# The second layer's activation as two ScalarE passes and one VectorE pass, without a maximum

## The chip, the cores and the metric

The kernel runs on one core of one Trainium2 chip. The metric is the device time of one execution in microseconds (us). Each time is that of a whole execution; the profiled execution also has a span, from its first to its last instruction.

## The reference

Three layers follow each other: an attention with pooled keys and values, and two layers that each multiply, apply an activation and multiply again. The change touches the activation of the last one:

```python
def _moe2_ref(x, w_in, w_out):          # x: 4608 x 512
    h = x @ w_in                        # w_in: 512 x 2048
    beta = 1.0
    neg = h <= -beta
    pos = h >= beta
    g = np.where(pos, h, np.where(neg, 0.0, (h + beta) ** 2 / (4.0 * beta)))
    return (g @ w_out).astype(np.float32)   # w_out: 2048 x 512
```

So g is h above 1, zero below -1 and ((h + 1) / 2) squared between. Inputs and output are fp32; the weights of both layers come as 64-bit numbers and are turned into fp32 in the kernel.

## The kernel before

Every operand of a matmul is split into a high part, a copy rounded to the matmul's format (ScalarE), and a low part, source minus high part (VectorE); a product is then three matmuls: high by high, high by low, low by high. Attention and the first layer take the first 960 us or so, and the second layer's second product (w_out, L1080) the last 380. The change lies in the stage between them, `first_phase` of the class `Second`, which forms h = x @ w_in and g.

That stage splits the matrices into 2 x 2 blocks and forms the four blocks of h from seven products instead of eight. It runs over 6 panels p of 768 tokens and, in each, over 8 steps j of 128 columns from each half of w_in: 48 steps s, one per **cycle**. A cycle has seven **slots**, each with one product of six 128x384 matmuls (line 838), in the order 6, 1, 7, 5, 2, 4, 3. Products 6, 5 and 3 belong to step c, the other four to step c + 1.

Three PSUM banks collect them. **X** takes products 1 and 2 and is one block of h. **V** takes product 7, which is copied out as p7 (`p<-V`), and then product 4. **Y** starts as a copy of X after product 1; product 6 is added and the sum copied out as `q`; product 5 is added, and then VectorE forms the block **W** = Y + p7 in p7's tile (`p<-Y,p`, line 857); product 3 is added and Y is a block of h. VectorE forms the block V = V + q in q's tile (`q<-V,q`, line 857). So product 3 has to wait until W has been formed, with products 2 and 4 (two slots) between, and product 5 until q has been copied.

The activation of one 128x384 block runs in up to four steps, in one tile t: `act1` (ScalarE, line 871) forms max(h/2 + 1/2, 0), with the constant tile `half` as bias. For X and Y, `act2` forms min(t, 1) times t on VectorE (line 877). For V and W, `act2` takes the minimum on GpSimd (line 879) and `act3` the square on ScalarE (line 884). `act4` (VectorE, line 890) takes the maximum of h and t, and the tile is stored to DRAM as g.

The order is written out by hand: after each slot's product, `after(c, slot)` issues its copies, adds and activation steps, and then a plan by cycle and slot issues the other work of that slot. That work is: the splits of the next panel's operands (`parts`, high part line 698, low part line 699) and the sums and differences of them (line 756), in the last three cycles of each panel and the first of the next (5 to 8, 13 to 16 and so on); and the splits of w_out's blocks (`w2o`), seven at a time over cycles 1 and 2, 3 and 4, 9 and 10, and so on up to 27 and 28. Every engine runs its instructions in this order, so one that waits holds all that are behind it. All transfers go through SyncE's queue, in the same order.

Of the kernel before, what the change touches and what calls it, by code (L numbers as in the profile page):

```python
# [8 lines left out]
F32 = mybir.dt.float32  # L9
F32R = mybir.dt.float32r  # L10
U32 = mybir.dt.uint32
AF = mybir.ActivationFunctionType
ALU = mybir.AluOpType
# [4 lines left out]
P = 128  # L18
# [17 lines left out]
def attention_moe_moe2(ctx: ExitStack, tc: tile.TileContext, qT, kT, v, k01, v01, w_in1, w_out1, w_in2, w_out2, out):  # L36
# [5 lines left out]
    nc = tc.nc  # L42
# [12 lines left out]
    const = ctx.enter_context(tc.tile_pool(name="const", bufs=1))  # L55
# [8 lines left out]
    ps_a = ctx.enter_context(tc.tile_pool(name="ps_a", bufs=2, space=PSUM))  # L64

    ident = const.tile([P, P], F32, name="ident")
    half = const.tile([P, 1], F32, name="half")
    mask = const.tile([96, 4], F32, name="mask")


# [128 lines left out]
    class Attention:  # L199
# [176 lines left out]
        def scores_early(self, blk, hf, ti, tag):  # L376
# [31 lines left out]
            for _ in range(4):  # L408
                next(parts)
# [257 lines left out]
    class Second:  # L667
# [26 lines left out]
            self.plan.setdefault((cycle, slot), []).append((f, args))  # L694


        def parts(self, hi, lo, src, engine=nc.vector):
            nc.scalar.activation(out=hi, in_=src, func=AF.Copy)
            engine.tensor_tensor(out=lo, in0=src, in1=hi, op=ALU.subtract)  # L699

        def w1_load(self, j):
            x, y = (raw_tile([P, DM], F32, f"w1{n}{j}") for n in "xy")
# [165 lines left out]
        def act1(self, what, s):  # L868
            if 0 <= s < self.STEPS:
                t = self.kept["t", what, s] = self.t_tile(f"t{what}{s}")  # L870
                nc.scalar.activation(out=t, in_=self.h_of(what, s), func=AF.Relu, scale=0.5, bias=half)  # L871

        def act2(self, what, s):
            if 0 <= s < self.STEPS:
                t = self.kept["t", what, s]
                if what in "XY":
                    nc.vector.scalar_tensor_tensor(out=t, in0=t, scalar=1.0, in1=t, op0=ALU.min, op1=ALU.mult)
                else:
                    nc.gpsimd.tensor_scalar(out=t, in0=t, scalar1=1.0, scalar2=None, op0=ALU.min)  # L879

        def act3(self, what, s):
            if 0 <= s < self.STEPS:
                t = self.kept["t", what, s]
                nc.scalar.activation(out=t, in_=t, func=AF.Square)

        def act4(self, what, s):
            if not 0 <= s < self.STEPS:
                return
            t = self.kept.pop(("t", what, s))
            nc.vector.tensor_tensor(out=t, in0=self.h_of(what, s), in1=t, op=ALU.max)  # L890
            p, j = divmod(s, self.NJ)
            c = 2 * NH * p + (NH if what in "YW" else 0)
            nc.sync.dma_start(out=self.g[j + (self.NJ if what in "VW" else 0)][:, c:c + NH], in_=t)
# [52 lines left out]
        def after(self, c, slot):  # L946
            if slot == 0:
                self.copy("q", "Y", c)
                self.act3("W", c - 1)
                self.act2("X", c)  # L950
                self.act4("V", c - 1)
            elif slot == 1:
                self.copy("Y", "X", c + 1)
                self.act1("Y", c - 1)
                self.add("V", "V", "q", c)
                self.act4("W", c - 1)
            elif slot == 2:
                self.copy("p7", "V", c + 1)
                self.act4("X", c)
                self.act2("Y", c - 1)  # L960
            elif slot == 3:
                self.act1("V", c)
                self.act2("V", c)
                self.add("W", "Y", "p7", c)
                self.act4("Y", c - 1)
            elif slot == 4:
                self.act1("W", c)
                self.act2("W", c)
            elif slot == 5:
                self.act1("X", c + 1)  # L970
                self.act3("V", c)


        def w2_fetch(self, t):
            self.w2 = getattr(self, "w2", {})
# [186 lines left out]

    with tc.manual_schedule():
        make_identity(nc, ident)
        nc.vector.memset(half, 0.5)
        nc.vector.tensor_reduce(
            out=mask, in_=ident[0:96, 0:96].rearrange("p (g c i) -> p c g i", g=3, c=4), axis=AX.XY, op=ALU.add
        )
# [248 lines left out]
```

## Time and profile before

| | us |
|---|---|
| median of 3 runs | 1729.06 |
| lowest and highest of them | 1723.62, 1729.28 |
| the profiled execution, its own time | 1726.16 |
| its span | 1723.8 |
| mean granted TensorE clock, as a share of full speed | 0.994 |

The engines are TensorE (PE, with its weight loads as PEld, which overlap the matmuls), VectorE (DVE), ScalarE (ACT), GpSimd (POOL) and SyncE (SP, which issues the transfers). A row of a timeline gives the start and the length in us, the engine, the line of the kernel, the tile written and the tiles read with the numbers left out, the shapes, and in brackets how long the engine was idle before it and what ended that wait. Two instructions of one engine may overlap a little, so a row can end after the next one begins.

### The profile page before, as it was taken

What the parts mean: (1) busy time and instruction counts of PE and PEld (TensorE: products, weight loads), DVE (VectorE), ACT (ScalarE), POOL (GpSimd) and SP (SyncE); (2) the same over time, 40 slices, a digit from 0 to 9 for tenths busy, and PEclk for the clock granted to TensorE, in tenths of its full rate; (3) what the DMA queues carried; (4) which work ended last, traced back from release to release, by engine and by line L of the source; (5) the groups of instructions that cost most, each with busy time, mean ns of one, the idle gap of its engine ahead of it and who ended that gap; (6) DMA issues with size and microseconds to landing.
All of it is one profiled execution on the core that took longest, in us unless ns stands there. A gap on an engine that the chain in (4) does not pass through costs nothing.

```text
span 1723.8 us, 27635 instructions
## 1 busy us (share of the span) xinstructions
PE 1663.2 (96%) x9372; PEld 1475.6 (86%) x9372; DVE 1144.2 (66%) x2192; ACT 868.3 (50%) x1873; POOL 562.1 (33%) x648
## 2 busy tenths in 40 slices
PE   6789999999999999999999999999999899999998
PEld 4578878788878888888888889889999799999998
DVE  7968745545555454544436677877775788887967
ACT  4646533444444444443335667767676454444444
POOL 3533311112111111111124354554543524252535
PEclk9999999999999999999999999999999899999999
DMA  6425333232232323222131356456336874435231
GB/s 215 152 73 171 102 101 120 83 97 79 71 111 66 97 88 98 70 69 74 53 104 44 125 200 223 170 196 222 129 138 209 296 269 141 140 124 163 83 111 62
DMA packets 154221, 221.50 MB, mean 128 GB/s; under 512 B 18592, under 2 KB 95392, under 8 KB 154080
## 3 DMA queue, kind: packets, MB, share of 16 engines
q1 hardware_dynamic: 154080, 219.73, 39.1%
q8 instruction: 74, 1.21, 0.3%
q14 instruction: 67, 0.55, 0.1%
HBM read 136.84 MB, written 82.84 MB: 127 GB/s over the span
## 4 chain that ended last, share of the span: by engine, by line
PE 77%; DVE 10%; DMA 5%; issue 3%; ACT 2%; POOL 1%; SPq 0%; DVEq 0%; POOLq 0%; ACTq 0%
PE u L1080 21%; PE acc L622 7%; PE acc L623 7%; PE acc L624 7%; PE h L595 7%; PE h L596 7%; PE h L597 7%; PE Y L838 4%; PE X L838 2%; PE V L838 2%; PE sc L419 2%; PE tm L475 1%; DMA g<-tV 1%; DVE xs L699 1%; DMA w2d<-w2o 1%
## 5 line engine op out<-in xcount | busy, mean ns | idle before, releaser
L1080 PE MATMUL u<-v,m 128*128 128x256 f32 x3024 | 368.1, 285 | 6.6 <-DVE m L1045 6.6
L1080 PEld LDWEIGHTS u<-v,m 128*128 128x128 f32 x3024 | 366.8, 193 | 8.0 <-DVE m L1045 7.7
L1045 DVE TENSOR_TENSOR m<-m,m 128x512 fp32r<-128x512 f32 (+1 forms) x280 | 248.6, 917 | 56.7 <-ACT m L1040 48.5
L1040 ACT ACTIVATE m<-m 128x512 fp32r<-128x512 f32 (+1 forms) x280 | 162.8, 588 | 191.2 <-PE u L1080 134.4
L132 DVE TENSOR_TENSOR gl<-t,gh 128x512 fp32r<-128x512 f32 x136 | 98.0, 720 | 227.1 <-ACT gh L130 221.2
L622 PE MATMUL acc<-gh,w0o 128*128 128x512 f32 x576 | 231.2, 401 | 0.0
L596 PE MATMUL h<-xl,w0i 128*128 128x512 f32 x576 | 225.5, 392 | 4.9 <-DVE xl L181 4.1
L595 PE MATMUL h<-xh,w0i 128*128 128x512 f32 x576 | 229.3, 398 | 0.3 <-DMA xh<-xk 0.3
L623 PE MATMUL acc<-gl,w0o 128*128 128x512 f32 x576 | 225.4, 391 | 0.0
L597 PE MATMUL h<-xh,w0i 128*128 128x512 f32 x576 | 225.2, 391 | 0.0
L624 PE MATMUL acc<-gh,w0o 128*128 128x512 f32 x576 | 225.1, 391 | 0.0
L606 ACT ACTIVATE t<-h 128x512 f32<-128x512 f32 x144 | 86.0, 597 | 249.5 <-PE h L597 154.0
L596 PEld LDWEIGHTS h<-xl,w0i 128*128 128x128 f32 x576 | 108.5, 188 | 27.8 <-DVE xl L181 4.9
L622 PEld LDWEIGHTS acc<-gh,w0o 128*128 128x128 f32 x576 | 108.4, 188 | 23.8 <-issue 2.6
L595 PEld LDWEIGHTS h<-xh,w0i 128*128 128x128 f32 x576 | 108.5, 188 | 23.5 <-DMA xh<-xk 1.1
L624 PEld LDWEIGHTS acc<-gh,w0o 128*128 128x128 f32 x576 | 108.4, 188 | 23.3
L597 PEld LDWEIGHTS h<-xh,w0i 128*128 128x128 f32 x576 | 108.4, 188 | 22.7
L623 PEld LDWEIGHTS acc<-gl,w0o 128*128 128x128 f32 x576 | 108.6, 189 | 20.5
L452 POOL TENSOR_TENSOR at<-at,r 128x32 f32<-128x32 f32 (+3 forms) x160 | 68.8, 450 | 136.7 <-DVE r L449 119.3
L879 POOL TENSOR_SCALAR tV<-tV 128x384 f32<-128x384 f32 x48 | 58.1, 1211 | 151.8 <-ACT tV L871 126.1
L838 PE MATMUL Y<-xs,v 128*128 128x384 f32 x432 | 88.0, 341 | 9.0 <-DVE p L857 8.3
L130 ACT ACTIVATE gh<-t 128x512 fp32r<-128x512 f32 x144 | 91.0, 632 | 4.4
(272 smaller groups left out, 3045.5 us busy)
## 6 DMA issues: line engine op xcount, KB each, us to landing
m<-g SPq DMA_DIRECT2D x128, 256.0 KB
w2d<-w2o SPq DMA_DIRECT2D x56, 256.0 KB
v<-w2d SPq DMA_DIRECT2D x28, 512.0 KB
x<-o SPq DMA_DIRECT2D x36, 256.0 KB
xr<-x SPq DMA_DIRECT2D x24, 384.0 KB
g<-tX SPq DMA_DIRECT2D x48, 192.0 KB
g<-tV SPq DMA_DIRECT2D x48, 192.0 KB
g<-tW SPq DMA_DIRECT2D x48, 192.0 KB
```

The lines of the kernel that those rows point to most:

```text
L130: nc.scalar.activation(out=hi, in_=src, func=AF.Copy)
L132: engine.tensor_tensor(out=lo, in0=src, in1=hi, op=ALU.subtract)
L595: nc.tensor.matmul(ph, wh[:, c], xh, start=k == 0, stop=False)
L596: nc.tensor.matmul(ph, wh[:, c], xl, start=False, stop=False)
L597: nc.tensor.matmul(ph, wl[:, c], xh, start=False, stop=k == KT - 1)
L622: nc.tensor.matmul(acc, wh[:, c], gh, start=st, stop=False)
L623: nc.tensor.matmul(acc, wh[:, c], gl, start=False, stop=False)
L624: nc.tensor.matmul(acc, wl[:, c], gh, start=False, stop=sp)
L838: nc.tensor.matmul(ps, w[:, c], x[k, i], start=begin and k == n == 0, stop=k == 1 and n == 2, skip_group_check=True,)
L1040: nc.scalar.activation(out=self.s[u][0], in_=self.unit_source(u), func=AF.Copy)
L1045: nc.vector.tensor_tensor(out=lo, in0=self.unit_source(u), in1=hi, op=ALU.subtract)
L1080: nc.tensor.matmul(ps, a[:, c], w, start=begin and i == 0, stop=f == self.NJ - 1 and i == 2, skip_group_check=True,)
```

## The change

The activation takes the same three steps for all four blocks. `act1` is a Prelu on ScalarE with slope 1/2 below zero of h - 1, which gives h - 1 above 1 and (h - 1)/2 below. `act2` is a Relu on ScalarE of that plus 1, in place: h above 1, and (h + 1)/2, not under zero, below. `act3` is min(t, 1) times t on VectorE: h above 1, and the square below. The biases are constants in the instruction, so the tile `half` goes. The maximum with h is gone, and with it the last read of h after `act1`. The GpSimd minima and the ScalarE squares of V and W are gone too. `act3` and the store stand where `act4` stood; X's second step moves from VectorE to ScalarE in the same slot, and V's and W's second step stands behind their first on ScalarE. `parts` loses a parameter that no call gave.

```diff
-        def parts(self, hi, lo, src, engine=nc.vector):
+        def parts(self, hi, lo, src):
             nc.scalar.activation(out=hi, in_=src, func=AF.Copy)
-            engine.tensor_tensor(out=lo, in0=src, in1=hi, op=ALU.subtract)
+            nc.vector.tensor_tensor(out=lo, in0=src, in1=hi, op=ALU.subtract)
...
-                nc.scalar.activation(out=t, in_=self.h_of(what, s), func=AF.Relu, scale=0.5, bias=half)
+                nc.scalar.activation(out=t, in_=self.h_of(what, s), func=AF.Prelu, alpha=0.5, bias=-1.0)

         def act2(self, what, s):
             if 0 <= s < self.STEPS:
                 t = self.kept["t", what, s]
-                if what in "XY":
-                    nc.vector.scalar_tensor_tensor(out=t, in0=t, scalar=1.0, in1=t, op0=ALU.min, op1=ALU.mult)
-                else:
-                    nc.gpsimd.tensor_scalar(out=t, in0=t, scalar1=1.0, scalar2=None, op0=ALU.min)
+                nc.scalar.activation(out=t, in_=t, func=AF.Relu, bias=1.0)

         def act3(self, what, s):
-            if 0 <= s < self.STEPS:
-                t = self.kept["t", what, s]
-                nc.scalar.activation(out=t, in_=t, func=AF.Square)
-
-        def act4(self, what, s):
             if not 0 <= s < self.STEPS:
                 return
             t = self.kept.pop(("t", what, s))
-            nc.vector.tensor_tensor(out=t, in0=self.h_of(what, s), in1=t, op=ALU.max)
+            nc.vector.scalar_tensor_tensor(out=t, in0=t, scalar=1.0, in1=t, op0=ALU.min, op1=ALU.mult)
...
             if slot == 0:
                 self.copy("q", "Y", c)
-                self.act3("W", c - 1)
+                self.act3("V", c - 1)
                 self.act2("X", c)
-                self.act4("V", c - 1)
             elif slot == 1:
...
-                self.act4("W", c - 1)
+                self.act3("W", c - 1)
             elif slot == 2:
                 self.copy("p7", "V", c + 1)
-                self.act4("X", c)
+                self.act3("X", c)
                 self.act2("Y", c - 1)
             elif slot == 3:
...
-                self.act4("Y", c - 1)
+                self.act3("Y", c - 1)
...
             elif slot == 5:
                 self.act1("X", c + 1)
-                self.act3("V", c)
```

VectorE in cycle 15, before, from X's first VectorE pass to the add that forms W (t of block and step is `tX15` and so on, `q15` is V's tile, `p715` is W's, `xs17` an operand of the next panel):

```order
L877 SCALAR_TENSOR_TENSOR tX15_10605<-tX15_10605 128x384
L890 TENSOR_TENSOR tV14_10577<-q14_10532,tV14_10577 128x384
L699 TENSOR_TENSOR xs17_10628<-xr2_01_10422,xs17_10628 128x384
L857 TENSOR_TENSOR q15_10622<-V15_10556,q15_10622 128x384
L890 TENSOR_TENSOR tW14_10591<-p714_10476,tW14_10591 128x384
L699 TENSOR_TENSOR xs17_10628<-xr2_11_10426,xs17_10628 128x384
L890 TENSOR_TENSOR tX15_10605<-X15_10538,tX15_10605 128x384
L877 SCALAR_TENSOR_TENSOR tY14_10640<-tY14_10640 128x384
L857 TENSOR_TENSOR p715_10563<-Y15_10545,p715_10563 128x384
```

The same stretch of VectorE now, from V's pass to the add that forms W:

```order
L881 SCALAR_TENSOR_TENSOR tV14_10547<-tV14_10547 128x384
L698 TENSOR_TENSOR xs17_10596<-xr2_01_10396,xs17_10596 128x384
L856 TENSOR_TENSOR q15_10591<-V15_10526,q15_10591 128x384
L881 SCALAR_TENSOR_TENSOR tW14_10561<-tW14_10561 128x384
L698 TENSOR_TENSOR xs17_10596<-xr2_11_10400,xs17_10596 128x384
L881 SCALAR_TENSOR_TENSOR tX15_10575<-tX15_10575 128x384
L856 TENSOR_TENSOR p715_10533<-Y15_10515,p715_10533 128x384
```

Eight instructions stood ahead of the add and six stand there now; X's and Y's L877 have gone from it, and Y's last pass follows behind the add as Y's maximum did.

ScalarE before, from W's first pass in cycle 14 to the copy of product 7 in cycle 15 (`Y16` is Y's bank, written with the copy of X):

```order
L871 ACTIVATE tW14_10591<-p714_10476,half_85 128x384
L698 ACTIVATE xs15_10596<-xr2_00_10420 128x384
L871 ACTIVATE tX15_10605<-X15_10538,half_85 128x384
L884 ACTIVATE tV14_10577<-tV14_10577 128x384
L698 ACTIVATE xs15_10596<-xr2_10_10424 128x384
L851 ACTIVATE q15_10622<-Y15_10545 128x384
L884 ACTIVATE tW14_10591<-tW14_10591 128x384
L698 ACTIVATE xs17_10628<-xr2_01_10422 128x384
L851 ACTIVATE Y16_10638<-X16_10631 128x384
L871 ACTIVATE tY14_10640<-Y14_10462,half_85 128x384
L698 ACTIVATE xs17_10628<-xr2_11_10426 128x384
L851 ACTIVATE p716_10654<-V16_10647 128x384
```

The same stretch of ScalarE now:

```order
L870 ACTIVATE tW14_10561<-p714_10448 128x384
L875 ACTIVATE tW14_10561<-tW14_10561 128x384
L697 ACTIVATE xs15_10566<-xr2_00_10394 128x384
L870 ACTIVATE tX15_10575<-X15_10508 128x384
L697 ACTIVATE xs15_10566<-xr2_10_10398 128x384
L850 ACTIVATE q15_10591<-Y15_10515 128x384
L875 ACTIVATE tX15_10575<-tX15_10575 128x384
L697 ACTIVATE xs17_10596<-xr2_01_10396 128x384
L850 ACTIVATE Y16_10606<-X16_10599 128x384
L870 ACTIVATE tY14_10608<-Y14_10434 128x384
L697 ACTIVATE xs17_10596<-xr2_11_10400 128x384
L850 ACTIVATE p716_10622<-V16_10615 128x384
```

V's and W's squares have left it; W's second pass stands directly behind its first, X's behind the copy q. Y's follows behind the copy of product 7, the last row. V's two passes stand ahead of this stretch.

## Rows read from the trace of the kernel before

**Rows 1.** The page: busy us of each engine, share of the span, instructions.

```profile
PE 1663.2 (96%) x9372; PEld 1475.6 (86%) x9372; DVE 1144.2 (66%) x2192; ACT 868.3 (50%) x1873; POOL 562.1 (33%) x648
```

**Rows 2.** Four stretches: their length, then busy us (instructions) of each engine.

```profile
core 0: us, PE busy (x) PEld busy (x) DVE busy (x) ACT busy (x) POOL busy (x), PEclk, DMA share, GB/s
1041.90:1057.50 15.60, 14.84 (x85) 14.52 (x85) 10.74 (x23) 11.03 (x27) 7.45 (x9) 1.00 0.66 236
969.80:1338.70 368.90, 352.59 (x1977) 341.02 (x1976) 272.18 (x517) 251.54 (x554) 175.49 (x160) 1.00 0.53 184
1242.30:1264.20 21.90, 21.90 (x129) 21.90 (x128) 12.23 (x25) 13.09 (x27) 7.00 (x6) 1.00 0.33 111
1089.00:1097.60 8.60, 7.85 (x43) 7.11 (x42) 8.49 (x16) 6.21 (x15) 4.43 (x5) 1.00 0.26 91
```

**Rows 3.** Stretches of the five panels' cycles 5 to 8, summed by the view.

```profile
sum 165.00, PE 152.92 PEld 144.84 DVE 135.15 ACT 113.87 POOL 84.67; mean PE 30.58 PEld 28.97 DVE 27.03 ACT 22.77 POOL 16.93
```

**Rows 4.** Waits from 969 to 1339: us in total, times, longest us.

```profile
ACT tW L871 <- DVE p L857: 40.2, 40, 2.5
...
PEld Y L838 <- DVE p L857: 22.7, 26, 1.6
...
ACT tV L884 <- POOL tV L879: 8.2, 11, 2.6
ACT xs L698 <- DMA xr<-x: 7.8, 6, 3.0
...
ACT tX L871 <- DMA g<-tV: 3.9, 4, 2.4
```

**Rows 5.** Groups by form: busy us, mean ns of one, idle before and its releasers.

```profile
L879 POOL TENSOR_SCALAR tV<-tV 128x384 f32<-128x384 f32 x48 | 58.1, 1211 | 151.8 <-ACT tV L871 126.1 <-DMA w2d<-w2o 20.3 <-DMA xr<-x 5.4
...
L890 DVE TENSOR_TENSOR tV<-q,tV 128x384 f32<-128x384 f32 x48 | 29.5, 614 | 0.0
L877 DVE SCALAR_TENSOR_TENSOR tY<-tY 128x384 f32<-128x384 f32 x48 | 29.4, 612 | 1.7 <-ACT tY L871 1.6
L871 ACT ACTIVATE tV<-q,half 128x384 f32<-128x384 f32 x48 | 29.2, 608 | 0.0
...
L871 ACT ACTIVATE tX<-X,half 128x384 f32<-128x384 f32 x48 | 27.2, 567 | 4.8 <-DMA g<-tV 3.9 <-PE X L838 0.7
...
L890 DVE TENSOR_TENSOR tX<-X,tX 128x384 f32<-128x384 f32 x48 | 26.4, 550 | 0.0
...
L884 ACT ACTIVATE tV<-tV 128x384 f32<-128x384 f32 x48 | 24.8, 516 | 8.2 <-POOL tV L879 8.2
...
L851 ACT ACTIVATE q<-Y 128x384 f32<-128x384 f32 x48 | 23.4, 487 | 36.3 <-PE Y L838 36.0
```

**Rows 6.** Timeline of VectorE in cycle 15.

```profile
1092.20 0.55 DVE L877 SCALAR_TENSOR_TENSOR tX<-tX 128x384 f32<-128x384 f32 x1
1092.67 0.55 DVE L890 TENSOR_TENSOR tV<-q,tV 128x384 f32<-128x384 f32 x1
...
1096.02 0.55 DVE L857 TENSOR_TENSOR p<-Y,p 128x384 f32<-128x384 f32 x1
```

**Rows 7.** Timeline of ScalarE at the end of cycle 14's work: V's square.

```profile
1090.75 0.53 ACT L884 ACTIVATE tV<-tV 128x384 f32<-128x384 f32 x1 [1.31 <-POOL tV L879]
```

**Rows 8.** Timeline of VectorE in cycle 14, beside GpSimd's panel sums.

```profile
1084.80 0.54 DVE L890 TENSOR_TENSOR tX<-X,tX 128x384 f32<-128x384 f32 x1
1085.27 0.90 DVE L877 SCALAR_TENSOR_TENSOR tY<-tY 128x384 f32<-128x384 f32 x1
```

**Rows 9.** Timeline of ScalarE in the first layer: a pass and one that needs it.

```profile
342.65 0.60 ACT L606 ACTIVATE t<-h 128x512 f32<-128x512 f32 x1 [1.25 <-issue]
343.27 0.63 ACT L130 ACTIVATE gh<-t 128x512 fp32r<-128x512 f32 x1
```

**Rows 10.** Groups by line on ScalarE: table loads in the whole span.

```profile
L323 ACT ACT_TABLE_LOAD x1 | 1.3, 1283 | 0.7 <-PEq L1404 0.7
```

**Rows 11.** Timeline of ScalarE in cycle 21, when panel 3 is prepared.

```profile
1145.09 0.52 ACT L698 ACTIVATE xs<-xr 128x384 fp32r<-128x384 f32 x1 [3.00 <-DMA xr<-x]
```

More of the change, by code (lines that the diff above doesn't have):

```diff
@@ L66, in attention_moe_moe2 @@
     ident = const.tile([P, P], F32, name="ident")
-    half = const.tile([P, 1], F32, name="half")
     mask = const.tile([96, 4], F32, name="mask")
@@ L1164, in attention_moe_moe2 @@
         make_identity(nc, ident)
-        nc.vector.memset(half, 0.5)
         nc.vector.tensor_reduce(
```

## Prediction

> **What bounds the kernel now.** I read the busy shares first, then a table of stretches, the table of waits, the costs by form, and last the timelines of single cycles. TensorE is busy 96% of the span [rows 1], so a change that touches no matmul can only win what TensorE loses, and it loses it in one stage. In the stage that the change edits, the product cycles of the second layer, 47 cycles take 368.9 us and the weight loads, which follow each other without a gap when TensorE is not held up, fill 341.0 of them [rows 2]: 27.9 us are idle. Three quiet cycles take 21.9 us with no idle time at all, 7.3 us each, and there VectorE has 12.2 us of work, ScalarE 13.1 and GpSimd 7.0 [rows 2]. So the floor is TensorE's 7.3 us, and in a quiet cycle every other engine has over 2.5 us to spare; nothing can be won there.
>
> The idle time lies in cycles that carry splits. The four cycles in each of five panels in which the next panel's operands are made take 165.0 us and hold 144.8 us of weight loads [rows 3]: 20.2 us idle. The other 7.7 us lie mostly in cycles that split the second product's weights, as in the pair of 15.6 us with 14.5 us of loads [rows 2]. The waits say who is late: TensorE waits 22.7 us in 26 waits for VectorE's L857, longest 1.6 [rows 4]. This is the add that makes W (`p<-Y,p`): product 3 may not write into Y's bank before it has read Y, and it has the two products between, some 2.1 us. It is late because VectorE is in order and has a backlog: in cycle 15 VectorE is busy 8.49 of 8.6 us [rows 2], and from X's L877 at 1092.20 to the add at 1096.02 its instructions stand end to end, 0.47 us apart [rows 6].
>
> **VectorE.** Per cycle the change takes out four maxima, two of 0.614 and two of 0.550 us, and two products of a minimum and a multiplication for X and Y, and adds four of the latter (L877, 0.612 or a little less) [rows 5]: eight instructions of the activation and its adds become six, -1.1 us of busy time. What counts is where they stood. The order shows that in cycle 15 eight instructions stood from X's first VectorE pass up to the add of W, and that now six do, from V's last pass on: X's and Y's first passes are gone from there, and Y's last pass comes behind the add. At 0.47 us apart [rows 6] the add can begin 0.94 us earlier. The 26 waits have a mean of 0.87 us and none is over 1.6 [rows 4]; with 0.94 off each, most vanish, and I estimate that some nine longer ones leave about 0.4 each, 3.5 us. So 19 us of the 22.7 go.
>
> One thing works against it: beside GpSimd's panel sums, X's maximum, which reads PSUM, took 0.54 us, and Y's pass, which reads only SBUF, 0.90 [rows 8]. X's last pass now reads SBUF too, and can be 0.35 us longer in the one or two cycles per panel with such sums: at most 3 us over ten cycles, inside the 3.5 left and the 4 below.
>
> **GpSimd.** 96 minima of 1.2 us go [rows 5], 115 us of an engine that is no bound. Its order matters in the panels: V's minimum queued behind six panel sums, and ScalarE stood 1.31 us in front of V's square in cycle 14 [rows 7]; there are 11 such waits, 8.2 us [rows 4]. Behind that square stood the high part of the next panel's operand, for which TensorE's product 7 waited next. The wait is gone and the sums start about 1.2 us earlier (W's minimum stood ahead of them). Since most of the 8.2 us was hidden behind VectorE's backlog, I count 1.5 us.
>
> **ScalarE.** Removed: four Relu with a tile as bias, 2 x (0.608 + 0.567), and two squares, 2 x 0.516, together 3.38 us. Added: four Prelu and four in-place Relu with constants as bias, whose form the trace does not show. Bounds for one: below, a copy from PSUM, 0.487, and an in-place square, 0.516; above, the Relu with a bias tile, 0.567 and 0.608 [rows 5]. I take the lower ones, since copy and square have no tile as bias either: 2 x 0.487 + 6 x 0.516 = 4.07, +0.69 us a cycle (+1.4 by the upper ones). V's and W's two passes stand back to back and the second needs the first: such a pair shows starts 0.62 apart for a first pass of 0.60 [rows 9], so they do not overlap, 0.1 us twice; together +0.9. In a quiet cycle that gives 4.4 + 0.9 = 5.3 of 7.3 us, which TensorE hides. In the pair of weight cycles it gives 11.0 + 1.8 = 12.8 of 14.6, in the panels 113.9 + 18 = 132 of 20 x 7.3 = 146 [rows 2, 3], hidden on average. In the cycle with most splits it is 6.2 + 0.9 = 7.1 of 7.3 [rows 2]: no room for a wait there, so the cover is thin. A fresh wait of ScalarE holds what stands behind it in the queue: X's first pass, the copy q that product 5 needs, and the high parts that VectorE's low parts need.
>
> Such waits exist and stay: for the panel's loads, 7.8 us in 6 waits, and for the store of an earlier V tile, 3.9 us in 4 [rows 4]; in panel 3's preparation ScalarE stood 3.00 us for a load [rows 11]. Stores, loads and their order on SyncE's queue don't change, and TensorE arrives earlier at them. I take back 2.5 us for that one panel and 1.5 for the other four, 4 us.
>
> The first pass is now a Prelu, in a stage that had none. In the whole span there is one table load, 1.283 us [rows 10], though the first layer's Prelu and attention's exponentials alternate and this stage runs Relu; so I count no load.
>
> At one point a rule speaks against the change. For 128x384 in fp32, ScalarE's square takes 0.516 us and VectorE's passes 0.550 to 0.614 [rows 5]: a pass costs the same on either. The Trainium skill, "ScalarE: Activation LUTs", section on rules for kernel authors, says to put relu, max, min and mul on VectorE, which it gives as up to about three times faster per element in bf16. By that rule ScalarE's load would grow by more than VectorE's shrinks, and the sum would be that of rival 3 below; by the rows ScalarE gains 0.9 us a cycle where VectorE loses 1.1, and the sum stands.
>
> **The last cycle and the rest.** After the last step nothing hides the chain q, product 5, W, product 3; one instruction fewer ahead of the add there gives 0.5 us. The first layer, attention and the second product are untouched; the constant tile that is dropped was one small fill at the start, nothing.
>
> **The sum.** -19 -1.5 -0.5 +4 = -17 us. The profiled execution has 1726.16 us, 2.4 around its span and 2.9 below the median of 1729.06. On it the forecast is 1709, on the median 1712; I say 1710.
>
> **Rivals.** (1) *Faster, as summed*, 1699 to 1720: at best all 27.9 us go, 1698 on this execution; at worst ScalarE's upper bounds and longer X passes leave 7. (2) *The panels are paced by their transfers*: loads and tile releases arrive when they did, ScalarE waits longer at them, and the panels keep their 20.2 us; of the 7.7 us outside some 6 go: 1720, within 0.5%. For it: the waits on transfers above. Against: 7.8 and 3.9 us over five panels are less than half of the 20.2, and VectorE is the one that is full. (3) *ScalarE becomes the bound*, slower: in the 28 cycles with splits its eleven passes and their high parts, all in one queue, fill the time between two adds of W. Each such cycle then grows by its added 0.9 us, 25 us, less the 8.2 us of waits on GpSimd that go: +17, 1743. It decides where ScalarE's work and its forced waits in a cycle pass the present length: for the fullest cycle 7.1 us of work plus 1.5 of waits against 8.6 now. For it: ScalarE stands 40.2 us, 40 times, for the add of W [rows 4], 1.0 us each, and now two dependent passes follow. Against: that wait shrinks with the add, and the panel average leaves 0.7 us a cycle.
>
> **Chances.** Forecast 0.75, (2) 0.15, (3) 0.10. The range of 8 in 10 takes the forecast's cases but the outermost and half of (2): 1699 to 1723. Half a per cent, 8.6 us, is about what a measurement of this kernel tells from no change; faster than that 0.75, within 0.15, slower 0.10.
>
> **What would show it.** Right: 47 cycles in 350 to 358 us; TensorE's waits for the add of W down from 22.7 to under 6 us; no wait of ScalarE on GpSimd's V; Prelu and Relu at 0.49 to 0.52 us; VectorE under 7.3 us in cycle 15. Wrong: the waits for W stay and VectorE in front of it waits for ScalarE's high parts or second passes (rival 3), or TensorE's waits move to the copy q and the new panel's operands with ScalarE standing on loads (rival 2), or the new passes take 0.6 us.

## The result and the profile after

The changed kernel takes **1703.64 us** (median of 4 runs, 1702.66 to 1704.40); the kernel before took 1728.84 in the runs beside it (4 runs, 1723.62 to 1729.28). The ratio is **0.9867, 95% interval 0.9854 to 0.9881**: 1.3% faster. The forecast was 1710 in a range of 1699 to 1723, so the direction and the range held, and the gain is 25 us where the sum said 17. Measured again later, the same kernel took 1706.53 beside 1727.63, ratio 0.9875 [0.9859, 0.9892].

The page of the profiled execution of after (1704.4 us, span 1702.6): busy us of each engine, beside [rows 1].

```profile
PE 1660.0 (97%) x9372; PEld 1478.9 (87%) x9372; DVE 1086.4 (64%) x2095; ACT 896.1 (53%) x1969; POOL 448.0 (26%) x552
```

VectorE has 58 us less work, GpSimd 114 less, ScalarE 28 more. The stretches of after that answer to [rows 2]: the 47 cycles, three quiet cycles, cycle 15, and the pair of weight cycles; length, then busy us (instructions) of each engine, then the granted clock.

```profile
core 0: us, PE busy (x) PEld busy (x) DVE busy (x) ACT busy (x) POOL busy (x), PEclk, DMA share, GB/s
973.90:1318.20 344.30, 344.23 (x1977) 341.81 (x1976) 216.69 (x423) 279.34 (x648) 64.94 (x66) 1.00 0.57 197
1216.10:1238.00 21.90, 21.90 (x129) 21.90 (x128) 8.96 (x18) 15.29 (x35) 0.00 (x0) 1.00 0.34 123
1083.90:1091.20 7.30, 7.30 (x44) 7.30 (x43) 6.52 (x14) 7.09 (x18) 0.00 (x0) 1.00 0.35 124
1040.10:1054.60 14.50, 14.50 (x85) 14.50 (x84) 8.56 (x19) 12.10 (x30) 3.52 (x4) 1.00 0.75 252
```

The five stretches of panel cycles 5 to 8 in after, summed by the view, beside [rows 3]:

```profile
sum 147.30, PE 147.23 PEld 145.25 DVE 110.76 ACT 128.00 POOL 35.62; mean PE 29.45 PEld 29.05 DVE 22.15 ACT 25.60 POOL 7.12
```

The 47 cycles went from 368.9 to 344.3 us, the panels in them from 165.0 to 147.3, the pair from 15.6 to 14.5; the quiet cycles stayed at 7.3 each, as they had to. Almost the whole gain of 25 us lies in this stage; the two profiled executions differ by 21.8 us, since the stages ahead of the 47 cycles, which the change does not touch, were 4.1 us longer in that of after. From here on the **loss** of a run is the length of its 47 cycles less 342.2 us, which is 47 times 7.28, the length of a cycle in which TensorE's weight loads follow each other without a gap: 26.7 before, 2.1 after.

The waits of after in this stage, beside [rows 4]: us in total, times, longest us.

```profile
POOL xr L755 <- DVE xs L698: 40.1, 3, 13.6
...
DVE p L856 <- PE Y L837: 18.7, 17, 1.1
...
ACT xs L697 <- DMA xr<-x: 2.8, 5, 1.0
...
ACT tX L870 <- DMA g<-tV: 2.1, 1, 2.1
...
PEld Y L837 <- DVE p L856: 1.5, 6, 0.4
```

TensorE's wait for the add that makes W was 22.7 us in 26 waits and is 1.5 in 6. The pair has turned round: VectorE now waits 18.7 us for TensorE before that add. No wait of ScalarE for GpSimd's V is left, since there is no such pass. GpSimd, without the minima, is idle most of the time. Groups of after by form, beside [rows 5]: busy us, mean ns of one, idle before.

```profile
L881 DVE SCALAR_TENSOR_TENSOR tX<-tX 128x384 f32<-128x384 f32 x47 | 30.5, 649 | 0.0
...
L881 DVE SCALAR_TENSOR_TENSOR tV<-tV 128x384 f32<-128x384 f32 x47 | 26.4, 562 | 0.4 <-ACT tV L875 0.4
...
L875 ACT ACTIVATE tV<-tV 128x384 f32<-128x384 f32 x47 | 24.7, 526 | 1.5
...
L870 ACT ACTIVATE tV<-q 128x384 f32<-128x384 f32 x47 | 24.4, 518 | 0.0
...
L870 ACT ACTIVATE tX<-X 128x384 f32<-128x384 f32 x47 | 22.3, 475 | 2.2 <-DMA g<-tV 2.1
```

ScalarE's first pass (L870) takes 0.475 to 0.518 us and its second (L875) 0.52 to 0.53, close to the lower of the two bounds in the prediction. A quiet cycle has 15.29 / 3 = 5.1 us of ScalarE work, cycle 15 has 7.09 of 7.30: the forecast had 5.3 and 7.1.

**When the panel's sums run** is a difference that none of those tables shows. GpSimd makes six sums for each panel. Its timeline around cycle 14, in the kernel before (that cycle's first weight load starts at 1080.20): start, us, instruction.

```profile
1080.68 1.17 POOL L879 TENSOR_SCALAR tW<-tW 128x384 f32<-128x384 f32 x1 [0.86 <-DVE xs L699]
1081.81 2.65 POOL L756 TENSOR_TENSOR xr<-xr 128x384 f32<-128x384 f32 x2
...
1086.99 2.29 POOL L756 TENSOR_TENSOR x2s<-xr,xr 128x384 f32<-128x384 f32 x2
```

And in after (first weight load at 1076.48):

```profile
1074.73 1.01 POOL L755 TENSOR_TENSOR xr<-xr 128x384 f32<-128x384 f32 x1 [13.14 <-DVE xs L698]
1077.18 1.26 POOL L755 TENSOR_TENSOR xr<-xr 128x384 f32<-128x384 f32 x1 [1.44 <-DMA g<-tW]
...
1080.66 2.62 POOL L755 TENSOR_TENSOR x2s<-xr,xr 128x384 f32<-128x384 f32 x2
```

Before, the sums stood behind W's minimum, began 1.6 us into the cycle and ended 9.1 us in, in the next cycle. After, the first starts 1.75 us ahead of the cycle and the last ends at 6.8. Counted from the start of the cycle, the sums begin over 3 us and end 2.3 us earlier. What that is worth took most of the experiments.

### The profile page after: what moved, and what is told of

Its sections match the earlier page's. It is cut to its first block, busy times and chain, and to the rows that moved or that the text cites. A ratio compares the mean times of both kernels' runs of the same rounds, so it can differ in the third digit from the quotient of the medians.

```text
span 1702.6 us, 27338 instructions
## 1 busy us (share of the span) xinstructions
PE 1660.0 (97%) x9372; PEld 1478.9 (87%) x9372; DVE 1086.4 (64%) x2095; ACT 896.1 (53%) x1969; POOL 448.0 (26%) x552
## 4 chain that ended last, share of the span: by engine, by line
PE 88%; DVE 5%; DMA 4%; ACT 1%; issue 1%; POOL 0%; SPq 0%; DVEq 0%; POOLq 0%; ACTq 0%
PE u L1068 20%; PE Y L837 8%; PE acc L621 8%; PE acc L622 7%; PE acc L623 7%; PE h L594 7%; PE h L595 7%; PE h L596 7%; PE X L837 5%; PE V L837 5%; PE sc L418 2%; PE tm L474 1%; DVE m L1033 1%; PE av L492 1%; PE av L494 1%
## 5 line engine op out<-in xcount | busy, mean ns | idle before, releaser
L596 PEld LDWEIGHTS h<-xh,w0i 128*128 128x128 f32 x576 | 108.6, 189 | 22.7
L837 PE MATMUL X<-xs,v 128*128 128x384 f32 x432 | 86.5, 334 | 0.0
```

Source lines behind the costliest of these rows:

```text
L596: nc.tensor.matmul(ph, wl[:, c], xh, start=False, stop=k == KT - 1)
L837: nc.tensor.matmul(ps, w[:, c], x[k, i], start=begin and k == n == 0, stop=k == 1 and n == 2, skip_group_check=True,)
```

## The experiments

The first question was which half of the change brings the gain: X and Y, whose maxima left VectorE (the prediction's term of 19 us), or V and W, whose minima left GpSimd (its term of 1.5). The diffs of this section are cuts against the changed kernel, and those of the first two leave out renamed methods.

### X and Y alone

V and W go back to the old form, with GpSimd's minimum, a square and a maximum.

```diff
-                nc.scalar.activation(out=t, in_=self.h_of(what, s), func=AF.Prelu, alpha=0.5, bias=-1.0)
+                if what in "XY":
+                    nc.scalar.activation(out=t, in_=self.h_of(what, s), func=AF.Prelu, alpha=0.5, bias=-1.0)
+                else:
+                    nc.scalar.activation(out=t, in_=self.h_of(what, s), func=AF.Relu, scale=0.5, bias=half)
...
+                    nc.gpsimd.tensor_scalar(out=t, in0=t, scalar1=1.0, scalar2=None, op0=ALU.min)
...
+                nc.scalar.activation(out=t, in_=t, func=AF.Square)
...
+                nc.vector.tensor_tensor(out=t, in0=self.h_of(what, s), in1=t, op=ALU.max)
```

> The change for blocks X and Y alone; V and W keep GpSimd's minimum, ScalarE's square and the maximum. VectorE loses its two passes ahead of the add that forms W, GpSimd keeps its 96 minima. Theory A (the gain is VectorE's shorter queue ahead of that add): most of the 25 us, 1707 to 1713, the rest being the panels' waits behind GpSimd. Theory B (the gain is the work taken off GpSimd, its queue and its place beside VectorE): at most 8 us, 1720 to 1727.

Measured 1724.17 us (10 runs, 1720.38 to 1728.71; before beside it 1726.84), ratio 0.9983 [0.9968, 0.9998]: hardly anything. The 47 cycles take 364.3 us, a loss of 22.2. What the prediction leads to, theory A, failed; the time lies in the range of theory B. The waits of this run in the 47 cycles:

```profile
DVE tV L896 <- ACT tV L887: 27.5, 28, 3.2
...
PEld Y L838 <- DVE p L857: 12.8, 21, 1.3
...
ACT tV L887 <- POOL tV L882: 12.7, 13, 3.0
```

Its ScalarE timeline at V's square, the instruction that waits for GpSimd's minimum (cycle 14 starts at 1086.95, cycle 15 at 1095.31):

```profile
1097.43 0.52 ACT L887 ACTIVATE tV<-tV 128x384 f32<-128x384 f32 x1 [1.72 <-POOL tV L882]
```

VectorE has 40 us less to do than before (232.1 busy) and TensorE gains 4.5: the time saved became VectorE's wait for V's square, 27.5 us, which waits for the minimum, which stands behind the six sums on GpSimd. The add for W is queued behind all this.

### V and W alone

The reverse: X and Y get their square, minimum and maximum back, V and W keep the new form.

```diff
+                if what in "VW":
+                    nc.scalar.activation(out=t, in_=self.h_of(what, s), func=AF.Prelu, alpha=0.5, bias=-1.0)
+                else:
+                    nc.scalar.activation(out=t, in_=self.h_of(what, s), func=AF.Relu, scale=0.5, bias=half)
...
+                if what in "XY":
+                    nc.vector.scalar_tensor_tensor(out=t, in0=t, scalar=1.0, in1=t, op0=ALU.min, op1=ALU.mult)
```

> The change for blocks V and W alone; X and Y keep their two VectorE passes, so eight VectorE instructions still stand ahead of the add that forms W, and GpSimd's 96 minima are gone. Theory A: 2 to 7 us, 1722 to 1727. Theory B: most of the gain, 1705 to 1711. If the two halves together give less or more than the whole, the halves share a wait.

Measured 1716.62 us (5 runs, 1712.46 to 1718.52), ratio 0.9937 [0.9915, 0.9958], 47 cycles 354.7, loss 12.5. Neither expectation holds; it lies between. But the half that was given 1.5 us brings 14.2, with VectorE almost as busy as before (261.5 us against 272.2, and the same 11.0 instructions a cycle). What is left of the waits for the add of W:

```profile
PEld Y L838 <- DVE p L857: 9.5, 10, 2.8
```

Alone the halves bring 4.5 and 14.2 us of the 47 cycles, together 24.6: 5.9 more than their sum. With one half done, the wait that the other half removes still holds the add.

Single cycles tell the halves apart. Here a cycle is counted from its first weight load to the next one's. Cycle 15 in the kernel before, with X and Y alone and with V and W alone (columns as in the first table of stretches):

```profile
1088.95:1097.62 8.67, 7.92 (x43) 7.18 (x43) 8.54 (x16) 6.28 (x16) 4.50 (x5) 1.00 0.26 93
```

```profile
1095.31:1104.02 8.71, 8.14 (x44) 7.11 (x44) 8.03 (x14) 6.92 (x18) 4.75 (x5) 1.00 0.26 92
```

```profile
1091.08:1098.36 7.28, 7.28 (x44) 7.28 (x44) 7.00 (x15) 6.42 (x16) 0.00 (x0) 1.00 0.31 110
```

With V and W alone, eight VectorE instructions still stand ahead of the add, and cycle 15 loses nothing: what the prediction read there as VectorE's backlog goes with V's and W's form. Cycle 14 is another matter: 8.75, 8.36 and 8.63 us, so neither half alone brings it near the floor. The cycles with weight splits lose 7.3 us before, 4.9 with X and Y alone and 1.1 with V and W alone: 6.2 of the 14.2 us lie where GpSimd makes no sums for a panel.

### One more VectorE pass for V and for X

To price VectorE's queue by itself, the changed kernel gets two extra passes a cycle that change no value.

```diff
+            if what in "VX":
+                nc.vector.scalar_tensor_tensor(out=t, in0=t, scalar=1e30, in1=t, op0=ALU.min, op1=ALU.max)
```

> The whole change, and one more VectorE pass, which leaves its values as they are, directly ahead of V's and of X's last pass in every cycle: eight instructions again ahead of the add that forms W, all else as after. Theory A: the loss comes back, 1717 to 1726. Theory B: VectorE's queue was not the cause, 1704 to 1707.

Measured 1720.97 us (10 runs, 1718.02 to 1725.40), ratio 0.9970 [0.9953, 0.9987], 47 cycles 362.6, loss 20.4: as expected. The wait comes back where the prediction saw it:

```profile
PEld Y L837 <- DVE p L856: 16.9, 19, 3.1
```

So instructions ahead of the add do cost what the prediction said, 18 us for two, but only where nothing else makes VectorE late. Cycle 15 takes 7.4 us even so; cycle 14 takes 8.9. The term was a fair price, put on a case in which other waits stood behind this one.

### GpSimd's pass back in V's and W's chain

The changed kernel with one GpSimd pass on V's and W's tile that changes no value, ahead of VectorE's last pass. ScalarE has nothing to wait for here.

```diff
+                if what in "VW":
+                    nc.gpsimd.tensor_scalar(out=t, in0=t, scalar1=1e30, scalar2=None, op0=ALU.min)
```

> The whole change, and a GpSimd pass on V's and W's tile, which leaves its values as they are, between ScalarE's second pass and VectorE's last: the 96 GpSimd instructions of 1.2 us are back, with VectorE but not ScalarE waiting for them. Theory A: VectorE waits only where the pass queues behind the panels' sums, 1706 to 1713. Theory B: most of the loss comes back, 1717 or more.

Measured 1716.87 us (5 runs, 1714.83 to 1718.81), ratio 0.9947 [0.9924, 0.9970], 47 cycles 356.9, loss 14.8: over theory A's range and just under theory B's. Its waits:

```profile
DVE tV L883 <- POOL tV L877: 19.9, 24, 1.1
...
PEld V L837 <- DVE xs L698: 7.7, 8, 2.3
...
PEld Y L837 <- DVE p L856: 4.8, 10, 1.1
```

TensorE now waits mostly for low parts of the panel (`xs`), less for the add. Two readings were open: VectorE stands behind the pass that waits for GpSimd (the 19.9 us), or the sums come late, since they stand behind W's pass again (2.2 to 9.6 us into cycle 14).

### A busier GpSimd that nobody waits for

Six 128x128 passes a cycle on a tile that is not needed any more, where the minima stood.

```diff
+                if what in "VW":
+                    for _ in range(3):
+                        nc.gpsimd.tensor_scalar(out=ident, in0=ident, scalar1=1.0, scalar2=None, op0=ALU.min)
```

> The whole change, and at the places of the old minima three 128x128 GpSimd passes each on a tile that nothing else uses any more: GpSimd is occupied as with the minima, the panels' sums start later, but no engine waits for these passes. Compare e4_pool, where the same places held a pass on V's and W's tile and the 47 cycles took 356.9 us, against 344.3 after. Theory C (VectorE's V pass stands in the queue behind GpSimd's sums): 344 to 347 us for the 47 cycles, 1703 to 1706 in all. Theory S (what costs is that the panels' sums start later, and the next panel's operands with them): 353 to 358, 1712 to 1718, with TensorE waiting for the low parts of the panel's operands in the third cycle of each panel.

Measured 1707.31 us (4 runs, 1702.59 to 1708.46), ratio 0.9878 [0.9845, 0.9911], 47 cycles 348.4, loss 6.3. The passes fill more of GpSimd than the minima did (GpSimd is busy 250.9 us in the 47 cycles, 175.5 before), yet cost 4.2. They need no data, so they run early and the sums keep their early place (cycle 14: the last ends 6.0 us in). GpSimd's load is thus not the cause. Both theories had supposed that these passes would make the sums late; they did not, so this run leaves the two readings open.

### Late sums without a wait

Here the sums are late and no instruction of the activation waits for GpSimd. Five 128x128 passes read W's sum as soon as it is there and write the unneeded tile; the panel's sums stand behind them. They are the only addition to the changed kernel.

```diff
+                if what == "W":
+                    h = self.kept["h", what, s]
+                    for k in range(5):
+                        nc.gpsimd.tensor_scalar(out=ident, in0=h[:, P * (k % 3):P * (k % 3) + P], scalar1=1.0, scalar2=None, op0=ALU.min)
```

> The changed kernel with five passes of GpSimd, 128x128 each, per cycle, which read W's sum as soon as VectorE has made it and write a tile that nobody needs any more; nobody waits for them, but they stand ahead of the panel's six sums on GpSimd, where W's minimum stood in the kernel before. So the sums begin about 2 us into the cycle and end after 8.9 us, as in the kernel before and in e4_pool (9.0 to 9.6), and no instruction of ScalarE or VectorE waits for V's or W's pass. Theory S (what the minima cost is that the panel's sums come late, and with them VectorE's part of the sums and the low parts): 47 cycles in 353 to 358 us, TensorE waits 6 to 9 us for low parts, 1713 to 1718 us. Theory C (what they cost is that ScalarE and VectorE, in order, stand behind an instruction that waits for GpSimd's pass; e4_pool had both): 47 cycles in 345 to 350 us, 1704 to 1709 us.

Measured 1713.14 us (6 runs, 1710.34 to 1715.88), ratio 0.9916 [0.9898, 0.9935], 47 cycles 357.0, loss 14.8, the same as with the pass in the chain. Theory S holds; theory C, by which these passes cost next to nothing, falls. That the two losses are equal is in part chance: cycle 15 loses 2.0 us here and 1.6 there, cycle 14 nothing here and 0.4 there. GpSimd around cycle 14, which starts at 1077.53:

```profile
1076.64 3.48 POOL L879 TENSOR_SCALAR ident<-p 128x128 f32<-128x128 f32 x5 [4.76 <-DVE p L856]
1080.08 2.64 POOL L755 TENSOR_TENSOR xr<-xr 128x384 f32<-128x384 f32 x2
...
1085.28 2.30 POOL L755 TENSOR_TENSOR x2s<-xr,xr 128x384 f32<-128x384 f32 x2
```

The sums run from 2.6 to 10.0 us in. VectorE makes the last two sums of the panel itself and waits for GpSimd's, and TensorE's waits in the 47 cycles are the low parts (7.8 in the two rows below, and 2.2 for low parts in tiles of other names) and the add:

```profile
PEld V L837 <- DVE xs L698: 6.4, 4, 2.0
...
PEld Y L837 <- DVE p L856: 4.6, 7, 1.5
...
PEld Y L837 <- DVE xs L698: 1.4, 3, 0.5
```

Late sums alone cost 14.8 - 2.1 = 12.7 us, and 11.4 against the second profile of the changed kernel, whose loss is 3.4. This is the upper end of what their lateness was worth, since they are later here than in the kernel before. VectorE's two sums there, in the cycle 15 that starts at 1088.95, and here, where it starts at 1084.82:

```profile
1089.62 1.32 DVE L756 TENSOR_TENSOR xr<-xr,x2s 128x384 f32<-128x384 f32 x2
```

```profile
1086.64 1.92 DVE L755 TENSOR_TENSOR xr<-xr,x2s 128x384 f32<-128x384 f32 x2 [0.91 <-POOL x2s L755]
```

They end 2.0 us into cycle 15 before, 2.3 with X and Y alone and 3.7 here, and that cycle loses 1.4, 1.4 and 2.0 us; in after and with V and W alone they end 1.2 and 0.8 us in, and it loses nothing. The 7.4 us between this run and X and Y alone (22.2) go with the form of V and W on the other engines: 4.3 of them in the cycles with weight splits, 3.0 in the panels' cycles. ScalarE's 12.7 us of waiting for the minimum is what the trace shows of it; no run undid that wait alone. One side effect of the added passes: twice, 2.6 us in all, ScalarE's copy q waits until they have read the tile it writes, in cycles with weight splits, which lose only 0.6 us here.

### How thin ScalarE's cover is

One more ScalarE pass a cycle (on W), and two (on W and Y), that change no value:

```diff
+                if what == "W":
+                    nc.scalar.activation(out=t, in_=t, func=AF.Relu)
```

> The whole change, and one more ScalarE pass per cycle, which leaves its values as they are, behind W's second: 0.5 us more work for ScalarE in every cycle. After, ScalarE has 7.1 of 7.3 us in the fullest cycle and 25.6 of 29.5 per panel. If ScalarE is still hidden on average: 0 to 4 us, 1703 to 1708. If it is the bound in every cycle with splits: 28 cycles by 0.4 to 0.5 us, 11 to 14 us, 1715 to 1718.

Measured 1709.96 us (4 runs, 1707.91 to 1712.99), ratio 0.9900 [0.9874, 0.9925], 47 cycles 350.4, loss 8.2: one pass costs 6.1, between the two expectations.

```diff
+                if what in "WY":
+                    nc.scalar.activation(out=t, in_=t, func=AF.Relu)
```

> The same with two more ScalarE passes per cycle, behind W's and behind Y's second: 1.0 us a cycle. By the work in the panels, 25.6 + 4 of 29.1 us, the panels are then past the floor: 5 to 14 us, 1709 to 1718. If ScalarE had been the bound already: twice what one more pass costs, 22 to 28 us, 1726 to 1732. If it has room for that too: 1703 to 1707.

Measured 1723.22 us (10 runs, 1719.51 to 1727.74), ratio 0.9973 [0.9959, 0.9986], 47 cycles 364.1, loss 22.0: two passes cost 19.9 and nearly the whole gain, again between two expectations. The waits of the run with two:

```profile
DVE xs L698 <- ACT xs L697: 22.5, 32, 2.7
...
PEld Y L837 <- DVE p L856: 15.0, 23, 1.2
...
PEld Y L837 <- ACT xs L697: 3.1, 3, 1.0
```

VectorE is hardly busier than in after (218.3 us against 216.7) and TensorE waits 15.0 us for its add again: VectorE stands in front of it, waiting for ScalarE's high parts. This is the mechanism of rival 3, half a microsecond a cycle away. In cycle 15 after has 7.09 us of ScalarE work in 7.30; one pass more makes 7.6. The loss shows one cycle later: cycle 15 still takes 7.28 us in both runs, and cycle 16 loses 1.0 us with one pass and 2.0 with two, where TensorE waits for a high part that ScalarE has not reached, for its low part and, with two passes, for the add. With two passes the cycles with weight splits lose 5.6 us as well (0.4 with one).

### A version that beats both

With the stage near its floor, the largest gap left in after, behind the start, is TensorE's 4.0 us at the change to the second product. It waits for a low part, and VectorE stood 4.8 us before it could write that part, until the store of a Y tile, which had held the place, was done:

```profile
1335.55 0.69 DVE L1033 TENSOR_TENSOR m<-m,m 128x512 fp32r<-128x512 f32 x1 [4.81 <-DMA g<-tY]
```

That store stood in SyncE's queue behind four loads. The first edit turns the rotation of the activation's tiles by one, so that the places needed first hold earlier tiles, and issues four loads behind the last stores.

```diff
-            pool, tag = ((g_p, "gh"), (raw_p, "raw"), (g_p, "gl"))[self.n_t % 3]
+            pool, tag = ((raw_p, "raw"), (g_p, "gh"), (g_p, "gl"))[self.n_t % 3]
...
-                self.put(end, 4, self.g_load, 0, (2, 1), f + 4)
...
+            for f in range(4):
+                self.g_load(0, (2, 1), f + 4)
```

> The whole change, and two edits where the second product begins. There TensorE stood 4.0 us after the change, as 4.2 before it, for a part whose place is freed only when the last Y tile has been stored, and that store waited in the queue behind four loads. Now these four loads stand behind the last stores, and the three pools from which the activation's tiles come in turn are turned by one, so that the places that the second product needs first hold earlier tiles. If that store was the cause: 3 to 5 us faster than after, 1698 to 1701. If the loads, now later, take its place: no change, 1702 to 1705.

Measured 1701.42 us (4 runs, 1699.27 to 1704.27), ratio 0.9850 [0.9823, 0.9877]; the part behind the stage (the second product, from 1323.0 in after) fell from 379.6 to 375.8 us. For the runs that follow, the changed kernel was measured again beside them:

> The changed kernel once more, as the measure for the two runs beside it. Every theory expects 1702 to 1706 us, and 343 to 348 us for the 47 cycles.

It gave 1706.53 us (4 runs, 1702.88 to 1707.68) and 345.5 us for the 47 cycles. The median is half a microsecond over the expected range; the profiled execution's first stages, ahead of the 47 cycles, were 2.1 us longer than in the first profile. The first edit again:

> The loads of the second product's first groups are put into the tiles that come free first and are issued behind the last stores. Theory T (TensorE's 4.0 us at the change of parts are the loads that waited for the last store): the part behind the 47 cycles is 3 to 4 us shorter than in the changed kernel of the same call, and the median 2 to 4 us lower. Rival (the starts of the first stages, which differ by some 4 us between profiles, made the earlier 2 us): medians within 1 us of each other, although the part is shorter.

1698.94 us (4 runs, 1697.13 to 1702.54). The part is 375.7 us against 379.6 in after, as theory T expects; the median is 7.6 lower, more than the part explains. In the two profiled executions the part gives 3.9 and first stages that no edit touched 2.5, while the 47 cycles are 1.2 longer, 0.9 of it in one cycle near the end where ScalarE's copy q is late, behind a wait of 4.1 us for a store.

The second edit gives VectorE GpSimd's half of the sums in the second product's first groups.

```diff
-            tt = (nc.gpsimd if f % 2 or r == self.NPAIR2 - 1 else nc.vector).tensor_tensor
+            tt = (nc.vector if r == 0 and pos < 4 else nc.gpsimd if f % 2 or r == self.NPAIR2 - 1 else nc.vector).tensor_tensor
```

> As e10_tail1, and the half of the sums of the second product's first four groups that GpSimd made are made by VectorE. Theory T2 (behind the change of parts TensorE is held up by VectorE's passes that run slower beside GpSimd's sums): VectorE's passes there go back to about 0.6 us, and the part is another 1 to 3 us shorter than in e10_tail1. Rival (VectorE then has all the sums in one queue and becomes the bound there): the part is as long as in e10_tail1 or up to 2 us longer.

**1696.80 us** (4 runs, 1694.62 to 1698.26), ratio 0.9825 [0.9810, 0.9840]; the part is 370.3 us, 5.4 shorter than with the first edit alone: theory T2, with more than the 1 to 3 us expected. Stretches of the changed kernel's second profile: the first 45 us of the part, and 4 us each in the gap and behind it.

```profile
1326.30:1371.30 45.00, 38.95 (x286) 37.32 (x285) 37.96 (x42) 19.91 (x37) 22.28 (x13) 0.92 0.85 316
...
1336.30:1340.30 4.00, 0.74 (x3) 0.74 (x4) 1.49 (x3) 0.10 (x1) 0.66 (x1) 0.82 1.06 399
1340.30:1344.30 4.00, 4.00 (x21) 4.00 (x20) 4.00 (x4) 2.20 (x4) 2.77 (x3) 0.50 1.05 395
```

The first 45 us with the first edit:

```profile
1325.10:1370.10 45.00, 39.94 (x318) 38.51 (x317) 40.64 (x49) 21.22 (x39) 24.25 (x15) 1.00 0.95 348
```

And with both:

```profile
1322.20:1367.20 45.00, 43.92 (x362) 43.50 (x361) 41.03 (x65) 24.59 (x42) 11.19 (x4) 1.00 1.02 386
```

VectorE's low parts in these 45 us, with the first edit and then with both:

```profile
L1034 DVE TENSOR_TENSOR m<-m,m 128x512 fp32r<-128x512 f32 x30 | 28.9, 996 | 4.8 <-DMA g<-tV 3.2 <-ACT m L1029 1.6
```

```profile
L1034 DVE TENSOR_TENSOR m<-m,m 128x512 fp32r<-128x512 f32 x34 | 25.2, 753 | 4.4 <-DMA g<-tV 3.2 <-ACT m L1029 1.2
```

TensorE loads 285, then 317, then 361 weights in the 45 us. VectorE's low parts take 996 ns each with the first edit and 753 with both, as GpSimd's work there falls from 24.3 to 11.2 us; single ones take 0.69 us where GpSimd makes no sums and up to 1.78 where it does. Giving GpSimd's work to the engine that is late made that engine's own passes faster, and VectorE's busy time hardly grew (40.6 to 41.0 us) for 16 more instructions.

## Why the prediction came out as it did

The forecast was right in sign, in place and in most of what would show it: the gain is in the 47 cycles, outside the quiet ones; the wait for the add of W went; Prelu and Relu cost what a copy and a square cost; ScalarE's added time is hidden, if barely. The 47 cycles fell to 344.3, below the 350 to 358 given. That the range held is in part luck: the prediction put the waits that it counted down to one of two causes, and the change removes both. By its terms:

- **VectorE, -19.** The passes ahead of the add cost up to what was said once nothing else holds VectorE (18.3 us for the two extra passes, 10.4 for X and Y on top of V and W), but X and Y alone brought 4.5. The step that failed is the reading of the 22.7 us as one engine's backlog of instructions. What stood end to end in cycle 15 [rows 6] had arrived late, because GpSimd's sums had ended only in that cycle; with the sums in time and eight instructions ahead of the add, the cycle takes 7.28 us. When VectorE alone was relieved, the waits behind the late sums and behind V's square took over.
- **GpSimd and V's chain, -1.5.** Undersized by a factor of about ten: 14.2 alone, 20.1 on top of X and Y. The step named the right facts, V's square behind GpSimd [rows 7] and sums that start earlier, but put the start at 1.2 us earlier (over 3 in cycle 14) and took the value for hidden. Late sums alone cost up to 12.7. The reason there lies in queues in order: sums behind a minimum on GpSimd, VectorE's part of the sums and the low parts behind the sums, the add for W behind these. In the cycles with weight splits, 6.2 of the 14.2 and 4.5 of the 20.1, no run shows which wait of V's and W's old form it was.
- **The last cycle, -0.5.** 1.3 (6.2 to 4.9 us). The add for W begins 0.5 us earlier, as the term says. The other 0.8 is the last product: its six weight loads took 1.78 us before, at a granted clock of 0.50, and 0.99 after at 1.00, a change that the prediction did not have.
- **Transfers, +4.** Not there in the first profile. ScalarE waits 2.8 us for loads and 2.1 for the store, 7.8 and 3.9 before [rows 4]. Cycle 22, where panel 3 is prepared (by the count from weight loads the wait of [rows 11] lies in it, too), lost nothing there, but 1.3 to 1.8 us in most of the later profiles, the changed kernel's second among them (1.4), where ScalarE stood 2.0 to 2.4 us for the panel's load. So part of the 2.5 us for that panel is real. Rival 2 falls: the panels did not keep their idle time.
- **ScalarE's cost, nothing.** Right, with 0.2 us to spare in cycle 15; rival 3 needs one to two more passes, and then its mechanism is as described. Its price has a slip: by the plan 36 cycles carry splits (20 of the panels, 16 of the weights), not 28, so its own rule gives 36 x 0.9 - 8.2 = +24 us and not +17.
- **X's last pass from SBUF.** Longer as expected, 649 ns in the mean, and hidden but for what is in the 2.1 us left.

The sum was 8 us short: 4 for transfers that did not come, and about 4 because the two halves together brought the stage 24.6 us where the terms had 20.5.

The rule weighed there, of the Trainium skill, "ScalarE: Activation LUTs", section on rules for kernel authors, is that relu, max, min and mul belong on VectorE, with a factor given for bf16. For this shape and type the trace shows no such gain: a pass on 128x384 in fp32 took 0.475 to 0.526 us on ScalarE, and on VectorE 0.562 to 0.696 in the mean of a block, 0.55 where GpSimd made no sums.

## What to carry to other kernels

When an engine in order is full in one cycle, look where its work came from: a backlog can be another engine's lateness, and then thinning it out moves the wait and saves little. The place of an instruction in the queue of an idle engine can be worth more than its time: ask what stands behind it and in which cycle that must end. Gains of two edits that remove waits in one chain need not add up; measure each half and both.

## What the runs showed of the hardware

**VectorE beside GpSimd.** VectorE's timeline in cycle 14 of after, while GpSimd's sums run (1077.18 to 1083.28):

```profile
1078.90 0.92 DVE L881 SCALAR_TENSOR_TENSOR tW<-tW 128x384 f32<-128x384 f32 x1
1079.75 1.37 DVE L881 SCALAR_TENSOR_TENSOR tX<-tX 128x384 f32<-128x384 f32 x1
...
1082.33 0.55 DVE L856 TENSOR_TENSOR p<-Y,p 128x384 f32<-128x384 f32 x1
1082.80 0.90 DVE L881 SCALAR_TENSOR_TENSOR tY<-tY 128x384 f32<-128x384 f32 x1
```

The adds, one of whose operands is in PSUM, keep their 0.55 us; here passes with both operands in SBUF, even the same tile twice, take 0.90 to 1.37 instead of 0.55. The Trainium skill, "SBUF — State Buffer", section "Who interferes with whom", says that a VectorE instruction with two SBUF inputs contends with a GpSimd instruction that reads SBUF; the trace agrees. How much it costs depends on what GpSimd does: beside the one-input 128x128 passes of the run with late sums (0.63 to 0.88 us each in the mean) VectorE's passes on one tile took 0.54 to 0.65.

**The clock after a gap.** In the changed kernel's second profile TensorE idles 3.85 us at the change to the second product, and the granted clock is 0.82 in the stretch of the gap and 0.50 in the next 4 us, the lower of its two levels (1.2 of 2.4 GHz); with the first edit, where the gap is 1.3 us and a later one 1.9, it is 1.00 over the whole 45 us. It also fell without one long gap. The next row is the stretch of the last cycle's last product in the kernel before, behind two waits of TensorE's weight loads of 0.96 and 1.47 us; the one below it is the same in after, behind two of 0.90 and 1.00 us.

```profile
1343.10:1344.90 1.80, 1.75 (x5) 1.75 (x6) 1.66 (x3) 1.77 (x4) 1.62 (x2) 0.50 0.95 299
```

```profile
1322.10:1323.10 1.00, 0.96 (x5) 0.97 (x6) 0.59 (x2) 1.00 (x3) 0.00 (x0) 1.00 1.16 301
```

These rows give no rule by the length of a single gap.
